# Attention stores in one written order with the loads, turns in two other slots of a quad, and two tiles turned in the next layer

## The chip, the cores and the metric

The kernel runs on one core of a Trainium2 chip. The metric is the device time of one execution in microseconds (us), the median of several runs. A core has five engines with queues of their own: TensorE (PE, matmuls and transposes; PEld is its weight load), VectorE (DVE), ScalarE (ACT), GpSimd (POOL) and SyncE (SP, which here only issues DMAs). Results of PE land in PSUM, from where DVE and ACT copy them on.

## The reference

Two kinds of layer alternate on an x of 2048 rows and 640 columns, twice each:

```python
x = x + Re(DFT_seq(DFT_hidden(LN(x))))                # spectral, layer 0
x = x + (softmax(mask(q @ k.T * 20**-0.5)) @ v) @ wo  # attention, layer 0; q, k, v from LN(x) @ wqkv
x = ...spectral, layer 1;  x = ...attention, layer 1
```

Attention has 32 heads of 20 columns; a row sees itself and the 255 rows before it. The DFTs are matmuls with given cosine and sine matrices, of which only the real part is kept.

## The kernel before, in words

**Numbers.** Float32 values are held as two f16 parts, high and low; a product of two such values takes three matmuls (high·high, high·low, low·high).

**The program** is `spectral(0)`, `attention(0)`, `spectral(1)`, `attention(1)`. The 2048 rows make 16 tiles of 128. Attention works in 8 blocks of 256 queries (two tiles), each with 16 pairs of heads and two tiles, so 32 steps to a block and 256 to a layer. Four steps are a *quad* (four heads of both tiles). `attention` is written as one loop over g, the step (from L1220 on); r is its place in the block, 0 to 31.

**One step g** issues, in this order: `scores(g)` (PE into PSUM `sp`, then DVE a masked copy L1050 and a maximum L1054 into `m`); `by_key(g−7)` (the scores of an earlier step by key into `tp`, a sigmoid on ACT L1098 into `ptq`, masks on POOL); the loads of x rows for the norm of block b+2 at r = 4; `copy_tops` (ACT L1075); one step of a layer norm on DVE (`slow_step`; its last operation is L150, into `lny`, which ACT and POOL then split into `xs`); every fourth step `values` (PE into `pv`) and every fourth `back` (the quad's output, transposed back and divided, DVE L1146 and L1147, into `os` by POOL); and then *fill*.

**Fill** is a list of generators (`Unit`) that give one matmul at a time: the q/k projection of the next block (`proj_qk`), its v projection, the output projection of the block before last (`out_tile`), and at the end of layer 0 the first stage of the next spectral layer. `run_fill(ns)` issues matmuls worth ns nanoseconds. How many a step gets is a rate times a factor by g % 4 (1.12, 0.28, 1.3 and 1.3 for 0, 1, 2 and 3).

**Turns.** A tile must be transposed before it can be contracted. A *turn* is one Unit: `turned` (L941) issues five PE transposes into the PSUM bank `pt`, and then one copy out of it, by ACT (L950) for the high part (k = 0) and by DVE (L948) for the low part (k = 1). There are three kinds: `rows_turn` (a normed tile for the projections, `xs` to `early`), `out_turn` (an attention output, `os` to `ot`), and, in layer 0, `next_turn` (a finished, normed tile for the next spectral layer, `xs` to `xto`, which is then stored to `xud`). `turn_unit()` issues one whole turn. Before, it stands at the start of the fill of each step with g % 4 = 3 and, if fill and credit are over `TURN_ROOM` = 1000 ns, of each step with g % 4 = 0.

**One bank.** `pt` has one buffer. It is also what `hand_on` uses, at the very end of each step with g % 4 = 0: four transposes of the quad's maxima (`pt<-idh,tops`), which ACT copies in the next two steps.

**Order.** Inside attention, `tensor()` (L115) chains all PE instructions in written order, and `load()` (L164 to L171) chains the DMAs issued by SP in theirs. DMAs issued by ACT (`nc.scalar.dma_start`) are not in that chain: the stores of a finished tile to `x3d` (layer 0, `next_layer`, L896) or `out` (layer 1, `out_tile`, L880), and the store of a turned tile to `xud` (L956). SP's chain holds the stores of the projected q and k to `qkd`, the loads of the stacks `ks` and `qs` from there, and the loads of x rows (`x2d`). The q/k projection of a block ends at r = 20 to 23 of the block before; its stacks are loaded directly after.

**The seam.** In layer 0 the turns of tile 15 are not queued as fill. `attention` returns them as `hidden.rest`, and `spectral(1)` runs them beside its first products (one small step of each such generator after each product).

Of the kernel before, what the change touches and what calls it, by code (L numbers as in the profile page):

```python
# [19 lines left out]
NT = S // P  # L20
# [22 lines left out]
HAND_LAG = 4  # L43
# [3 lines left out]
M_UP = 2.0 ** 15  # L47
SHIFT = -20.0
TURN_STEPS = 8
TURN_ROOM = 1000  # L50
NORM_STEPS = (4, 9)
ROW_STEPS = 3
X_UP = 2.0 ** 10
# [8 lines left out]
def body(ctx: ExitStack, tc: tile.TileContext, x_in, cmat, whid, wqkv, wo, out):  # L62
    nc = tc.nc
# [35 lines left out]
    xu_d = [dram.tile([P, 2 * ND * P], F16, name=f"xud{i}") for i in range(NT)]  # L99
# [61 lines left out]
    def split(hi, lo, y, eng):  # L161
        nc.scalar.activation(hi, y, AF.Copy)
        eng.tensor_tensor(lo, y, hi, op=OP.subtract)
# [3 lines left out]
    def load(out, in_):  # L167
        with ExitStack() as order:
            if in_turn[0] and loads:
                order.enter_context(tc.issue_after(loads[-1]))  # L170
            i = nc.sync.dma_start(out, in_)  # L171
        loads.append(i.ins)
# [9 lines left out]
    def new_f():  # L182
        return pf_.tile([P, 512], F32, tag="f", name="pf", bufs=2)
# [578 lines left out]
    def attention(layer, proj, dst, final):  # L762
        with ExitStack() as st:
# [58 lines left out]
                yield 136  # L822

            def out_turn(i, k):
                if k == 0:
                    X2[i] = keep.tile([P, D], F32, tag="res", name="x3", bufs=4)
                    load(X2[i], x2_d[i])
                    OT[i] = sb.tile([P, 2, ND, P], F16, tag="ot", name="ot", bufs=2)
                yield from turned(OS[i // 2][:, :, i % 2], k, OT[i])
                done.add((i, k))  # L830
# [31 lines left out]
            def out_tile(i):  # L862
                ot = OT[i]
                x3 = x2 = X2.pop(i)
                for n in range(2):
                    cs = slice(n * 320, (n + 1) * 320)
                    pf = new_f()
                    k = 0
                    for dt in range(ND):
                        for l, r in ((0, 0), (0, 1), (1, 0)):  # L870
                            matmul(pf[:, :320], ot[:, l, dt], bo[r][:, dt, cs], start=k == 0, stop=k == 14)
                            k += 1
                            if k < 15:
                                yield 136
                    nc.vector.scalar_tensor_tensor(x3[:, cs], pf[:, :320], beta, x2[:, cs], op0=OP.mult, op1=OP.add)  # L875
                    if n == 0:
                        yield 136
                done.add((i, 2))
                if final:
                    nc.scalar.dma_start(dst[i], x3)  # L880
                else:
                    yield from next_layer(i, x3)

            slow, live = deque(), deque()

            def new_xs():

                while len(live) > 1:
                    for g in live.popleft():
                        for _ in g:  # L890
                            pass
                live.append([])
                return keep.tile([P, 2, D], F16, tag="xs", name="xs", bufs=2)

            def next_layer(i, x3):
                nc.scalar.dma_start(dst[i], x3)  # L896
                slow.append(next_norm(i, x3))
                yield from ()

            def next_norm(i, x3):  # L900
                ys = []
                yield from norm_steps([x3], ys)
                xs = new_xs()
                split(xs[:, 0], xs[:, 1], ys[0], nc.gpsimd)
                xt = keep.tile([P, 2, ND, P], F16, tag="xto", name="xto", bufs=2)
                live[-1].extend(next_turn(i, xs, xt, k) for k in range(2))
                if i < NT - 1:
                    fill.extend(Unit(now[0] + TURN_STEPS, g, "turn", now[0], [], True) for g in live[-1])

            def split_wo():  # L910
# [29 lines left out]
            def turned(xs, k, o, d0=0, d1=ND):  # L940
                pt = new_turn()  # L941
                ptv = pt.bitcast(F16)[:, :ND * P].rearrange("p (a b) -> p a b", a=ND)
                for dt in range(d0, d1):
                    transpose(ptv[:, dt], xs[:, k, dt * P:(dt + 1) * P], idh)
                    if dt < d1 - 1:
                        yield 56
                if k:
                    nc.vector.tensor_copy(o[:, k, d0:d1], ptv[:, d0:d1])  # L948
                else:
                    nc.scalar.activation(o[:, k, d0:d1], ptv[:, d0:d1], AF.Copy)  # L950
                yield 56

            def next_turn(i, xs, xt, k):
                yield from turned(xs, k, xt)
                if k:
                    nc.scalar.dma_start(xu_d[i], xt.rearrange("p a b c -> p (a b c)"))  # L956

            OS, OT, X2, done = {}, {}, {}, set()
            lastd = [0]
            credit = [0.0]  # L960
# [39 lines left out]
            def run_fill(ns):  # L1000
                credit[0] += ns
                while credit[0] > 0:
                    if unit[0] is None:
                        unit[0] = next_unit(False)
                        if unit[0] is None:
                            credit[0] = 0.0
                            break
                    if not step(unit[0]):
                        unit[0] = None
# [159 lines left out]
            NG = NT * NP  # L1169
# [30 lines left out]
            for g in range(NS):  # L1200
                now[0] = g
                b, r = divmod(g, 2 * NP)
                if g < NG:
                    if r == 0:
                        flush(("qk", b))
                        flush(("rows", b + 1))
                        if b < NBQ - 1:
                            queue_qk(b + 1)
                            queue_v(b + 1)
                    scores(g)  # L1210
                    if g % 4 == 3:
                        part_tops(g // 4)
                if 0 <= g - KEY_LAG < NG:
                    by_key(g - KEY_LAG)
                if g < NG and b < NBQ - 2:
                    if r == NORM_STEPS[0]:
                        x2s = [keep.tile([P, D], F32, tag="res", name="x2", bufs=4) for t in range(2)]
                        for t in range(2):
                            load(x2s[t], x2_d[2 * (b + 2) + t])
                    if r == NORM_STEPS[1]:  # L1220
                        slow.append(rows_norm(b + 2, x2s))
                if g < NG and r == VALUE_LAG:
                    flush(("v", b))
                    if b < NBQ - 2:
                        proj.new_rows(b + 2)
                    if b == NBQ - 1 and not final:
                        hidden = Hidden(xu_d)
                        hidden.load()
                        for k in range(2):
                            hidden.fetch(k)  # L1230
                            fill.append(Unit(g + NEXT_STEPS[k], hidden.stage(k, None), "next", NG + k))
                for pi in range(2):
                    n, m = divmod(g - HAND_LAG - 1 - pi, 4)
                    if m == 0 and 0 <= n < NG // 4:
                        copy_tops(n, pi)
                slow_step()
                n, m = divmod(g - VALUE_LAG, 4)
                if m == 0 and 0 <= n < NG // 4:
                    for part in range(2):
                        values(n, part)  # L1240
                n, m = divmod(g - BACK_LAG, 4)
                if m == 0 and 0 <= n < NG // 4:
                    back(n)
                rate = (total - spent[0] - credit[0]) / max(NG + FILL_LAST - g, 1)
                if g < NG and r < VALUE_LAG:
                    rate = max(rate, left(("v", b)) / (VALUE_LAG - r))
                if g < NG and r < QK_SLOT:
                    rate = max(rate, left(("v", b), ("qk", b + 1)) / (QK_SLOT - r))
                ns = max(rate, 400) * FILL[(g - VALUE_LAG + 2) % 4]
                m = (g - HAND_LAG) % 4  # L1250
                if m == 3 or m == 0 and credit[0] + ns > TURN_ROOM or g >= NG + HAND_LAG:
                    turn_unit()
                run_fill(ns)
                n, m = divmod(g - HAND_LAG, 4)
                if m == 0 and 0 <= n < NG // 4:
                    hand_on(n)
# [5 lines left out]
                    slow_step()  # L1262
            in_turn[0] = False
            if not final:
                hidden.rest = chain(*live[-1])
                return hidden

    hidden = Hidden(None)
    proj = spectral(0, [x_in[i] for i in range(NT)], hidden, True)
    hidden = attention(0, proj, x3_d, False)  # L1270
# [27 lines left out]
```

## Time and profile before

| | us |
|---|---|
| runs before | 2310.66, 2311.68, 2321.39 (median 2311.68) |
| profiled execution | 2304.6 |
| its span | 2302.9 (1.7 less) |
| mean granted PE clock | 0.985 of full speed |
| attention of layer 0 | about 600 to 1204 |
| spectral layer 1 | about 1215 to 1725 |
| attention of layer 1 | about 1725 to 2303 |

In a row of a timeline stand start, duration, engine, line, operation, output<-inputs, shape, type and count, and in brackets how long the engine was idle before it and what it waited for. A row of the waits names engine, output, line, the thing waited for, and then the total, the number of waits and the longest. In rows of windows stand start:end, length, the busy time of PE, PEld, DVE, ACT and POOL, the granted PE clock, and the DMA share and rate. L numbers are those of the kernel before.

### The profile page before, as it was taken

To read this page: it belongs to the slowest core of one execution; us is meant where nothing else is said; L and a number is where in the kernel's file an instruction comes from. 1 tells how busy PE (TensorE), PEld (TensorE's weight loads), DVE (VectorE), ACT (ScalarE), POOL (GpSimd) and SP (SyncE) were. 2 spreads that over 40 slices of the span, in tenths; PEclk is the share of its full clock that TensorE was granted. 3 is DMA by queue.
4 is the path that set the end of the run, shared out by engine and by line. 5 is a ranking of instruction groups with operands and counts; after the bars stand their busy time and mean duration, and the time that the engine had idled before them with its cause. 6 is when DMAs were issued, how large, how long until landed. Compare 5 with 4: busy or idle time off the path is not lost.

```text
span 2302.9 us, 55101 instructions
## 1 busy us (share of the span) xinstructions
PE 2135.0 (93%) x21985; PEld 1499.2 (65%) x21985; DVE 1695.3 (74%) x3601; ACT 1264.4 (55%) x2120; POOL 1365.2 (59%) x1773
## 2 busy tenths in 40 slices
PE   7989899999899999999889999999998999899997
PEld 5667566667566666666556777777665666666664
DVE  7887969777678788787656758585867777577664
ACT  5334344343477777777654433434325677667775
POOL 5675758658355565455446858585754555455443
PEclk9999999999999999999899999999999999999999
DMA  5864746354432332233324545363652322332230
GB/s 187 286 213 142 233 141 218 136 220 138 128 88 65 82 86 76 73 84 94 129 76 152 182 138 200 118 210 123 249 146 74 83 62 69 77 91 55 57 88 24
DMA packets 187606, 292.95 MB, mean 127 GB/s; under 512 B 13908, under 2 KB 120660, under 8 KB 178004
## 3 DMA queue, kind: packets, MB, share of 16 engines
q1 hardware_dynamic: 157108, 223.55, 32.9%
q10 hardware_dynamic: 30240, 65.88, 7.7%
q8 instruction: 172, 2.82, 0.5%
q14 instruction: 86, 0.70, 0.1%
HBM read 202.51 MB, written 86.87 MB: 126 GB/s over the span
## 4 chain that ended last, share of the span: by engine, by line
PE 64%; DVE 20%; DMA 5%; issue 5%; ACT 3%; POOL 2%; SPq 0%; DVEq 0%; ACTq 0%; POOLq 0%
PE pf L115 25%; PE y L115 9%; PE pv L115 8%; PE z L115 6%; PE x L115 6%; PE sp L115 5%; DVE cc L485 5%; DVE m L1054 3%; PE tp L115 3%; DVE sp L1050 2%; PE pt L115 2%; DMA qs<-qkd 1%; DVE res L508 1%; ACT ptq L1098 1%; DVE lnt L146 1%
## 5 line engine op out<-in xcount | busy, mean ns | idle before, releaser
L115 PEld LDWEIGHTS <-cc 128*128 128x128 f16 x5376 | 526.8, 98 | 243.0 <-issue 39.6
L1098 ACT ACTIVATE ptq<-tp,shift,alpha 128x768 f32<-128x768 f32 (+2 forms) x512 | 485.9, 949 | 200.8 <-PE tp L115 176.4
L115 PEld LDWEIGHTS <-big 128*128 128x128 f16 x4320 | 409.4, 98 | 136.1 <-issue 26.3
L1054 DVE TENSOR_REDUCE m<-sp 128x2 f32<-128x512 f32 (+1 forms) x512 | 345.0, 674 | 17.1
L1050 DVE COPY_PREDICATED sp<-mask,sp 128x256 f32<-128x256 int32 x448 | 190.9, 426 | 221.5 <-PE sp L115 207.3
L1103 POOL TENSOR_SCALAR_AFFINE_SELECT ptq<-ptq 128x512 f32<-128x512 f32 x224 | 145.3, 649 | 300.7 <-ACT ptq L1098 300.4
L115 PE MATMUL pf<-early,big 128*128 128x256 f16 x2400 | 304.6, 273 | 0.0
L482 ACT ACTIVATE cc<-cs 128x512 f16<-128x512 f32 x256 | 152.3, 623 | 253.5 <-POOL cs L475 103.9
L115 PE MATMUL y<-zc,cc 128*128 128x320 f16 x1728 | 266.6, 302 | 14.3 <-DVE pf L508 14.1
L115 PE MATMUL pf<-big 128*128 128x320 f16 x1680 | 241.2, 301 | 10.0 <-DVE zc L253 5.5
L485 DVE SCALAR_TENSOR_TENSOR cc<-cs,cc 128x512 f16<-128x512 f32 x256 | 233.6, 928 | 3.7 <-ACT cc L482 3.5
L485 DVE SCALAR_TENSOR_TENSOR cc<-cq,cc 128x512 f16<-128x512 f32 x192 | 203.1, 1059 | 0.0
L1105 POOL TENSOR_SCALAR_AFFINE_SELECT ptq<-ptq 128x512 f32<-128x512 f32 x256 | 163.2, 638 | 43.7 <-ACT ptq L1098 43.7
L115 PE MATMUL pv<-ptq,v 128*32 128x128 f32 (+1 forms) x3840 | 188.2, 336 | 0.0
L115 PE MATMUL z<-zc,cc 128*128 128x320 f16 x1152 | 177.8, 299 | 9.2 <-DVE res L508 9.2
L115 PE MATMUL sp<-ks,qs 62*128 62x256 f16 (+1 forms) x1792 | 155.3, 250 | 31.4 <-DVE m L1054 18.4
L115 PE MATMUL x<-zc,cc 128*128 128x320 f16 x1152 | 181.4, 301 | 0.0
L115 PE MATMUL pf<-big,early 128*128 128x320 f16 x960 | 159.9, 302 | 0.8 <-DVE x L875 0.8
L115 PE MATMUL tp<-qs,ks 62*128 62x128 f16 x2688 | 151.7, 218 | 3.4 <-ACT ptq L1098 3.0
L1075 ACT ACTIVATE qs<-pt 2x512 f16<-2x512 f16 x224 | 130.9, 585 | 39.7 <-PE pt L115 36.8
L115 PE MATMUL pf<-bo,ot 128*128 128x320 f16 x840 | 144.3, 304 | 6.7 <-DVE ot L948 6.5
L115 PEld LDWEIGHTS pv<-ptq,v 128*32 128x32 f32 x3840 | 109.3, 112 | 57.8 <-issue 4.5
(144 smaller groups left out, 3525.8 us busy)
## 6 DMA issues: line engine op xcount, KB each, us to landing
cq<-in_cmat_dram SPq DMA_DIRECT2D x64, 1024.0 KB
accd<-res ACTq DMA_DIRECT2D x96, 320.0 KB
res<-accd SPq DMA_DIRECT2D x96, 320.0 KB
x<-x2d SPq DMA_DIRECT2D x64, 320.0 KB
qkd<-early SPq DMA_DIRECT2D x160, 128.0 KB
ks<-qkd SPq DMA_DIRECT2D x108, 160.0 KB
qs<-qkd SPq DMA_DIRECT2D x84, 160.0 KB
x2d<-res ACTq DMA_DIRECT2D x32, 320.0 KB
```

Source lines behind the costliest of these rows:

```text
L115: i = getattr(nc.tensor, what)(*args, **kw)
L146: nc.vector.scalar_tensor_tensor(g, u, 1.5, g, op0=OP.add, op1=OP.mult)
L482: nc.scalar.activation(cc[m][:, 0], f, AF.Copy, scale=C_UP)
L485: nc.vector.scalar_tensor_tensor(cc[m][:, 1], f, C_UP, cc[m][:, 0], op0=OP.mult, op1=OP.subtract)
L508: marks["dve"] = nc.vector.scalar_tensor_tensor(o, z, Y_DOWN, f, op0=OP.mult, op1=OP.add).ins
L1050: nc.vector.copy_predicated(sp[:, :, 2 * P:3 * P], mask[:, None, :].to_broadcast([P, 2, P]), far)
L1054: topped[0] = nc.vector.tensor_reduce(TOP[g // 4][:, g % 4], sp[:, :, c0:3 * P], axis=AX.X, op=OP.max).ins
L1075: nc.scalar.activation(o, handed[n][rs].rearrange("r (i p) t -> r i p t", i=2), AF.Copy)
L1098: nc.scalar.activation(q[:, h:h + 2, a0 + first:a0 + 3], tp[:, :, first * P:3 * P].rearrange("p a (b c) -> p a b c", c=P), AF.Sigmoid, bia ...
L1103: nc.gpsimd.affine_select(out=q[:, :, a0], in_=q[:, :, a0], pattern=[[0, 4], [-1, P]], base=0, channel_multiplier=1, compare_op=OP.is_gt, ...
L1105: ins = nc.gpsimd.affine_select(out=q[:, :, a0 + 2], in_=q[:, :, a0 + 2], pattern=[[0, 4], [1, P]], base=0, channel_multiplier=-1, compare ...
```

## The change

It has four parts.

1. The stores to `x3d`, `out` and `xud` during attention go through `load()`, so SP issues them, in written order with the loads. 46 DMAs move from ACT to SP (16 to `x3d`, 16 to `xud`, 14 to `out`); the last two tiles of layer 1 are stored by ACT as before.
2. `turn_unit()` stands in each step with g % 4 = 2 or 3, between two halves of the step's fill. `TURN_ROOM` is gone.
3. `out_turn` takes its residual tile and loads it at k = 1, one turn later.
4. The turns of tile 14 are, like those of tile 15, not queued as fill but handed to the next spectral layer.

```diff
             def out_turn(i, k):
-                if k == 0:
+                if k:
                     X2[i] = keep.tile([P, D], F32, tag="res", name="x3", bufs=4)
                     load(X2[i], x2_d[i])
+                else:
                     OT[i] = sb.tile([P, 2, ND, P], F16, tag="ot", name="ot", bufs=2)
...
                 if final:
-                    nc.scalar.dma_start(dst[i], x3)
+                    load(dst[i], x3)
...
             def next_layer(i, x3):
-                nc.scalar.dma_start(dst[i], x3)
+                load(dst[i], x3)
...
-                if i < NT - 1:
+                if i < NT - 2:
                     fill.extend(Unit(now[0] + TURN_STEPS, g, "turn", now[0], [], True) for g in live[-1])
...
                 if k:
-                    nc.scalar.dma_start(xu_d[i], xt.rearrange("p a b c -> p (a b c)"))
+                    load(xu_d[i], xt.rearrange("p a b c -> p (a b c)"))
...
-                m = (g - HAND_LAG) % 4
-                if m == 3 or m == 0 and credit[0] + ns > TURN_ROOM or g >= NG + HAND_LAG:
+                if g % 4 in (2, 3) or g >= NG + HAND_LAG:
+                    run_fill(ns / 2)
                     turn_unit()
-                run_fill(ns)
+                    run_fill(ns / 2)
+                else:
+                    run_fill(ns)
...
-                hidden.rest = chain(*live[-1])
+                hidden.rest = chain(*live[0], *live[1])
```

Counted in the order in which PE's instructions are written, 33 steps have a turn directly ahead of `hand_on`'s transposes before, and none after. In the last block of layer 0, 9 steps have no fill matmul before (r = 10 to 18), and 14 after (r = 9 to 22); 31 fill matmuls come later there. The end of the q/k projection stays at r = 20 to 23 of a block.

DVE, layer 0, block 2, from the end of step 83 on, before; L1050 and L1054 are the score operations that come once in a step, `lny<-x` ends a norm, and `xto<-pt` empties the bank after a turn's low part:

```order
L150 TENSOR_SCALAR lny<-x_9266,lnmv,lnt 128x640
L1050 COPY_PREDICATED sp<-mask,sp 128x2x128
L1054 TENSOR_REDUCE m<-sp 128x2
L150 TENSOR_SCALAR lny<-x_9267,lnmv,lnt 128x640
L948 COPY xto<-pt 128x640
L1050 COPY_PREDICATED sp<-mask,sp 128x2x128
L1054 TENSOR_REDUCE m<-sp 128x2
```

The same place after:

```order
L149 TENSOR_SCALAR lny<-x_9272,lnmv,lnt 128x640
L1050 COPY_PREDICATED sp<-mask,sp 128x2x128
L1054 TENSOR_REDUCE m<-sp 128x2
L149 TENSOR_SCALAR lny<-x_9273,lnmv,lnt 128x640
L1050 COPY_PREDICATED sp<-mask,sp 128x2x128
L1054 TENSOR_REDUCE m<-sp 128x2
L1050 COPY_PREDICATED sp<-mask,sp 128x2x128
L1054 TENSOR_REDUCE m<-sp 128x2
L948 COPY xto<-pt 128x640
```

The copy has moved from the quad's first step, in which the maxima are handed on through the same bank, two steps on, to the third.

SP, layer 1, around the end of a block's q projection (`qkd_0` is its q, `qkd_1` the next k; `qs` and `ks` are the stacks; `x` are x rows), before:

```order
L171 DMA qkd_0_157<-early 128x2x256 x5
L171 DMA qs<-onesd_164 2x4096 x2
L171 DMA qs<-qkd_0_157 20x16x256 x6
L171 DMA x_29232<-x2d_86 128x640
L171 DMA x_29267<-x2d_93 128x640
L171 DMA x_29268<-x2d_94 128x640
L171 DMA qkd_1_160<-early 128x2x256 x3
```

The same place after:

```order
L170 DMA qkd_0_157<-early 128x2x256
L170 DMA x_28585<-x2d_85 128x640
L170 DMA qkd_0_157<-early 128x2x256 x4
L170 DMA qs<-onesd_164 2x4096 x2
L170 DMA qs<-qkd_0_157 20x16x256 x6
L170 DMA out_dram<-x_28585 128x640
L170 DMA x_29110<-x2d_86 128x640
L170 DMA x_29273<-x2d_93 128x640
L170 DMA x_29274<-x2d_94 128x640
L170 DMA out_dram<-x_29110 128x640
L170 DMA qkd_1_160<-early 128x2x256 x5
```

The stores of two finished tiles now stand among the loads, one directly behind the query stack, one ahead of the next block's k stores, and a residual tile's load has moved among the q stores.

DVE at the end of attention of layer 0, before; `lnt` and `lny` belong to the norms of tiles 14 (x_16994) and 15 (x_17209), `cc` to the conversion of the next layer's matrices, `big` and `zc` are results of its first stage:

```order
L150 TENSOR_SCALAR lny<-x_16994,lnmv,lnt 128x640
L146 SCALAR_TENSOR_TENSOR lnt<-lnt 128x1
L485 SCALAR_TENSOR_TENSOR cc<-cq,cc 128x512
L142 SCALAR_TENSOR_TENSOR lnt<-lnt 128x1
L485 SCALAR_TENSOR_TENSOR cc<-cs,cc 128x512
L146 SCALAR_TENSOR_TENSOR lnt<-lnt 128x1
L485 SCALAR_TENSOR_TENSOR cc<-cs,cc 128x512
L150 TENSOR_SCALAR lny<-x_17209,lnmv,lnt 128x640
L485 SCALAR_TENSOR_TENSOR cc<-cs,cc 128x512 x2
L948 COPY xto<-pt 128x640
L485 SCALAR_TENSOR_TENSOR cc<-cq,cc 128x512
L253 SCALAR_TENSOR_TENSOR big<-pf,big 128x320 x3
```

The same place after, from tile 14's norm (x_16974) on:

```order
L149 TENSOR_SCALAR lny<-x_16974,lnmv,lnt 128x640
L130 BN_AGGR lnmv<-lnst 128x2
L948 COPY xto<-pt 128x640
L134 TENSOR_SCALAR lnt<-lnmv 128x1
L252 SCALAR_TENSOR_TENSOR zc<-pf,zc 128x320
L135 TENSOR_SCALAR lnt<-lnt 128x1
L484 SCALAR_TENSOR_TENSOR cc<-cq,cc 128x512
L136 TENSOR_SCALAR lnt<-lnt 128x1
L137 TENSOR_SCALAR lnt<-lnt 128x1
L484 SCALAR_TENSOR_TENSOR cc<-cq,cc 128x512
```

Tile 14's norm ends ahead of the conversions `cc`, which stood ahead of it before, and no copy of tile 14 follows it there.

More of the change, by code (lines that the diff above doesn't have):

```diff
@@ L49 @@
 TURN_STEPS = 8
-TURN_ROOM = 1000
 NORM_STEPS = (4, 9)
```

## Prediction, made before the changed kernel ran

> **What bounds the kernel now.** The page's first lines and its chain of waits come first.
>
> ```profile
> span 2302.9 us, 55101 instructions
> PE 2135.0 (93%) x21985; PEld 1499.2 (65%) x21985; DVE 1695.3 (74%) x3601; ACT 1264.4 (55%) x2120; POOL 1365.2 (59%) x1773
> PE 64%; DVE 20%; DMA 5%; issue 5%; ACT 3%; POOL 2%; SPq 0%; DVEq 0%; ACTq 0%; POOLq 0%
> ```
>
> TensorE (PE) is busy for 93% of the span and no matmul is taken away. So the change can be worth only PE's idle time, 2302.9 − 2135.0 = 168 us over the whole program, and what PE does at a lower clock. Which of that idle time does it touch? The waits of PE in the attention of layer 0 (640 to 1120 us), columns: total, times, longest:
>
> ```profile
> PE pt L115 <- DVE xto L948: 9.5, 8, 2.3
> PE sp L115 <- DVE m L1054: 6.1, 11, 1.1
> PE pt L115 <- ACT early L950: 3.9, 7, 0.8
> PE pt L115 <- ACT xto L950: 2.2, 4, 1.3
> PE pt L115 <- ACT ot L950: 2.0, 4, 0.6
> PE pt L115 <- DVE ot L948: 0.9, 1, 0.9
> PE pt L115 <- DVE early L948: 0.7, 1, 0.7
> PE sp L115 <- DMA qs<-qkd: 0.5, 1, 0.5
> ```
>
> The largest group is the single PSUM bank `pt`: a turn's transposes or those of the maxima wait until the copy of the turn before has emptied it. In the attention of layer 1 (1740 to 2220 us) there are no `xto` turns, and other rows stand first:
>
> ```profile
> PE sp L115 <- DMA qs<-qkd: 7.3, 3, 5.6
> PE sp L115 <- DMA x<-x2d: 3.9, 1, 3.9
> PE pt L115 <- ACT early L950: 1.0, 4, 0.4
> ```
>
> There the scores of a block wait for its stack of queries. So the two layers have different limits beside PE's own work, and the change has a part for each. (±0.5% is 11.6 us here, about what a measurement of this kernel can tell from no change.)
>
> **The stores, layer 1.** The stall's place, the timelines of SP, ACT and PE and SP's waits:
>
> ```profile
> 1978.25 11.17 SPq L171 DMA_DIRECT2D qs<-qkd  x6
> 1983.88 0.34 ACTq L880 DMA_DIRECT2D out_dram<-x  x1
> SPq L171 <- DMA out_dram<-x: 8.8, 1, 8.8
> 1991.68 0.28 PE L115 MATMUL sp<-ks,qs 62*128 62x256 f16 x1 [1.31 <-DMA qs<-qkd]
> 1997.55 0.37 PE L115 MATMUL sp<-ks,qs 62*128 62x256 f16 x2 [5.59 <-DMA qs<-qkd]
> 2072.07 0.37 PE L115 MATMUL sp<-ks,qs 62*128 62x256 f16 x2 [3.95 <-DMA x<-x2d]
> 2131.89 2.75 SPq L171 DMA_DIRECT2D qs<-qkd  x6
> ```
>
> SP begins six loads at 1978.25 and needs 11.17 us to issue them, 8.8 of these waiting for the store of a finished tile, which ACT issues only at 1983.88, between sigmoids. At the undisturbed block boundary (last row) the same six take 2.75 us and no score waits. The loads don't read what the store writes; in the built program an SP transfer waits for the one before it on the same completion semaphore, and that one was ACT's. With the stores in SP's own written order, the store stands where its data are long ready and nothing on SP can wait for an issue that ACT is late with. The 7.3 and 3.9 us go: **−11.2 us** (ends 0 and −11.2). The loads end some 13 us before PE needs them (1978.25 to 1991.68) once they are issued without a pause, so nothing else is late next.
>
> The clock after these two stalls, in columns PE busy, PEld, DVE, ACT, POOL, granted clock, DMA share, GB/s:
>
> ```profile
> 1997.00:2001.00 4.00, 3.45 (x29) 2.36 (x29) 1.16 (x3) 1.47 (x2) 1.22 (x2) 0.50 0.31 118
> 2001.00:2006.00 5.00, 5.00 (x69) 2.84 (x63) 2.20 (x4) 3.39 (x6) 0.52 (x1) 0.80 0.01 3
> 2072.00:2077.00 5.00, 4.92 (x48) 3.19 (x52) 2.24 (x4) 3.15 (x4) 1.22 (x2) 0.50 0.19 70
> 2077.00:2082.00 5.00, 5.00 (x60) 3.02 (x53) 2.41 (x6) 2.78 (x5) 1.22 (x2) 0.89 0.00 0
> 1115.00:1140.00 25.00, 18.32 (x213) 11.10 (x211) 14.18 (x38) 14.24 (x19) 10.18 (x17) 0.73 0.53 216
> ```
>
> After the first stall 4 us pass at 0.50 and 5 at 0.80, a loss of 0.50×4 + 0.20×5 = 3.0 us of PE's work; after the second 0.50×5 + 0.11×5 = 3.05. Together 6.05 at most, if PE were all that counts there; DVE's share of the chain is 20%, so I take **−4** (0 to −6). The Trainium skill, "TensorE: Matmul & The Clock Gate", Part 1, says that the clock is halved after about 3.4 us without work and restored after about as long of busy time. The trace agrees in kind (0.50 behind waits of 5.59 and 3.95 us, 0.80 and 0.89 a window later), so these microseconds hang on the two stalls and not on the steps that show them.
>
> What speaks against this: the Trainium skill, "DMA: Bandwidth & Descriptors", section "Issuing engines are not separate DMA queues", says that DMAs of all issuing engines share the same 16 DMA engines and that the choice of engine only saves issue time on the sequencer. By that rule the two terms above are nothing; the trace has the 8.8 us wait on a store of the other engine against it. It makes a rival below. The issue time itself: 46 stores of 0.34 us (row 1983.88) leave ACT, 15.6 us, and come onto SP. ACT ends 3% of the chain and SP's issuing 0%, so I cost both at nothing.
>
> **The turns, layer 0.** Step 84 of layer 0, where the turn stands first in the step and the maxima's transposes last:
>
> ```profile
> 769.37 0.45 PE L115 MATMUL pt<-idh,xs 128*128 128x128 f16 x5
> 770.95 1.61 DVE L150 TENSOR_SCALAR lny<-x,lnmv,lnt 128x640 f32<-128x640 f32 x1
> 772.48 0.48 DVE L948 COPY xto<-pt 128x640 f16<-128x640 f16 x1
> 773.01 0.38 PE L115 MATMUL pt<-idh,tops 128*66 128x128 f16 x4 [2.34 <-DVE xto L948]
> ```
>
> The turn's five transposes end at 769.82. DVE gets to the copy only at 772.48, behind the block's norm, and PE waits 2.34 us with its whole queue: the next scores are written behind the maxima. In the new order no turn stands in a step that hands maxima on (33 such steps before, none after, counted in the written order); the copy has a step and more (some 1.8 us) before the bank is wanted. The rows of `xto`, `ot` and the one DVE row of `early` add to 9.5 + 2.2 + 2.0 + 0.9 + 0.7 = 15.3. The 3.9 of `early` by ACT partly stays, since turns of one block's rows are flushed one behind the other at block ends. Best end: 15.3 + 3.9 = −19. Worst end: waits come back at the new places, since now two turns stand in neighbouring steps (slots 2 and 3) and DVE's queue is no shorter: I put half of 15.3, −8. I take **−15**: what is late next is the score's PSUM bank (`DVE m`, 6.1 for 11 waits), and it is late in steps without turns already.
>
> **The last two tiles, the seam of the layers.** PE, DVE and ACT there:
>
> ```profile
> 1203.94 0.44 PE L115 MATMUL pt<-idh,xs 128*128 128x128 f16 x5
> 1208.73 0.69 DVE L485 SCALAR_TENSOR_TENSOR cc<-cq,cc 128x512 f16<-128x512 f32 x1
> 1210.17 0.74 ACT L162 ACTIVATE xs<-lny 128x640 f16<-128x640 f32 x1 [0.49 <-DVE lny L150]
> 1210.96 0.71 PE L115 MATMUL pt<-idh,xs 128*128 128x128 f16 x5 [4.98 <-DVE lnt L142]
> 1212.86 0.71 PE L115 MATMUL pt<-idh,xs 128*128 128x128 f16 x5 [1.19 <-POOL xs L163]
> 1214.77 0.29 PE L115 MATMUL pf<-idh,xs 128*128 128x128 f16 x1 [1.20 <-ACT xs L162]
> 1214.85 1.54 PE L115 MATMUL pf<-big 128*128 128x320 f16 x5
> ```
>
> PE transposes tile 14 by itself (waits of 4.98 and 1.19), then waits 1.20 for tile 15, and the products start at 1214.85. After the change no tile is turned behind 13; the first turn in the products' stretch needs tile 14's `xs` only, ready at 1210.17 + 0.74 = 1210.91. So the products start 1214.85 − 1210.91 = 3.9 us earlier, and tile 14's norm now stands ahead of the chunk conversions on DVE, of which one (0.69) was in front: 4.6 together, **−4.6** (0 if tile 15's norm ends last in either order; best −7.4, all three waits). Against it, tile 14's ten transposes now stand between products: 2 × 0.44 = **+0.9**.
>
> **What the moves cost.** Layer 0's last block has 14 steps without fill after, 9 before (counted in the written order); the 31 matmuls that these held are issued later. The window 1115 to 1140 us has the clock at 0.73: 0.27 × 25 = 6.75 us lost already. Five steps more of nine could lengthen that: **+2** (0, because the matmuls fill other gaps; +6, because the low clock doubles). The Trainium skill, same page as above, Part 4, says that transposes don't count as PE work for the clock gate. If so the steps with turns alone stay at the low clock; no run here shows it, and it would push this term to its upper end.
>
> The residual tile's load, one turn later, is wanted only behind the turn and 15 matmuls: 0 (up to +3, if a few of the 30 tiles wait).
>
> **Sum:** −11.2 − 4 − 15 − 4.6 + 0.9 + 2 = −31.9. Against the profiled execution of 2304.6 us (span 2302.9 and 1.7 around it) that is 2272.7; the median of the runs is 2311.68, 7.1 above the profiled one, and the same difference gives 2279.8, about 2280. With the terms at their best ends (−11.2 − 6 − 19 − 7.4 + 0.9) the difference is −42.7, 2269; with turns, seam and last block at their worst ends (−11.2 − 4 − 8 + 0.9 + 6) it is −16.3, 2295.
>
> **Rivals.** *A: SP's order holds loads back, slower.* A store in written order that waits for its data holds everything behind it on SP; in layer 0 the stores of turned tiles (`xud`) stand right ahead of the key loads of a block. If such a store waits more than the 13 us by which loads are early, scores wait: at each of 6 boundaries 5.6 us and 3.0 of clock, as measured for the one stall: 6 × 8.6 = +51.6, together −31.9 + 51.6 = +19.7, 2331. For it: exactly such a chain costs 8.8 us now. Against it: the store's data is a copy of 0.48 us behind a turn (row 772.48), 13 us is many steps, and layer 0's only wait on a query load is 0.5. *B: the stalls stay*, as by the rule above, since the loads share DMA engines with the same bytes: the first two terms fall, −31.9 + 15.2 = −16.7, 2295. Against it the two boundaries, 11.17 us with a late store and 2.75 without. *C: the turn waits change their name.* If DVE is what is late in these steps, PE waits at the next score for `m` instead of for `xto`; of the −15 only −3 stays: −19.9, 2292. For it DVE's 20% of the chain and 1.61 us for one norm operation in the row of step 84; against it, PE fills the time with fill matmuls that need no DVE. *D: nothing measurable*, turns and stores both only push the waits along: 2304 to 2312.
>
> **How the numbers follow.** Forecast 0.60; A 0.05, B 0.12, C 0.15, D 0.08. The likeliest case gives 2280. The range holds forecast, B and C: below, the sum of best ends, 2269, less the 1 us by which the two close runs differ: 2268; above, B with the turns at their worse end (−16.7 + 7 = −9.7), 2302. Left out are A, D and tails, about 2 in 10. Faster by over 0.5%: forecast, B and C, 0.87; within: D, 0.08; slower: A, 0.05.
>
> **What would show it.** Right: SP has no wait on `out_dram` and the six query loads of every boundary in layer 1 take about 3 us; PE's waits on `qs` in 1740 to 2220 are under 1 us and the clock stays high there; in layer 0 the rows `pt <- xto` and `ot` fall below 3 us together, with `DVE m` about as before; products start within some 2 us of tile 14's split. Wrong: waits on `ks` or `qs` in layer 0 (A), the 7.3 still there (B), `DVE m` grown by 10 (C), or a longer low-clock stretch at the end of either attention.

## The result, and the profile after

The changed kernel takes 2274.0 us (median of 4 runs, 2268.34 to 2283.0) beside 2311.17 for the one before: ratio 0.9848, 95% interval 0.9819 to 0.9877. Measured again beside some of its parts it took 2271.76 us, ratio 0.9816 (0.9790 to 0.9842). The profiled execution took 2268.34 us, 36.3 less than the 2304.6 of before; 31.9 less was forecast. Comparisons below leave disturbed runs out, and the profiled execution of one kernel (stores alone, clock 0.852) is not read for durations.

The page of after: PE does the same matmuls, in a shorter span. Its idle time is down from 168 to 2266.6 − 2131.3 = 135 us, its busy time by 3.7.

```profile
span 2266.6 us, 55134 instructions
PE 2131.3 (94%) x21985; PEld 1498.0 (66%) x21985; DVE 1699.9 (75%) x3601; ACT 1263.9 (56%) x2120; POOL 1364.0 (60%) x1773
PE 66%; DVE 21%; DMA 5%; issue 4%; ACT 2%; POOL 2%; SPq 0%; DVEq 0%; ACTq 0%; POOLq 0%
```

PE's waits after, layer 0, over the same steps as before (644.6 to 1112 us):

```profile
PE sp L114 <- DVE m L1054: 7.4, 18, 1.1
PE pf L114 <- DVE x L875: 5.9, 6, 1.2
PE tp L114 <- ACT ptq L1098: 2.7, 10, 0.4
PE pt L114 <- ACT early L950: 1.6, 3, 0.8
PE pf L114 <- DVE ot L948: 1.0, 1, 1.0
...
PE pt L114 <- DVE xto L948: 0.5, 1, 0.5
PE pt L114 <- DVE early L948: 0.5, 1, 0.5
```

The bank `pt` has gone from the head of the list: `xto`, `ot` and `early` together from 19.2 to 2.6 us. A new row stands second, fill that waits for the output projection's result (`x`, L875) to be read from its PSUM buffer.

The same for layer 1 (1726 to 2186 us):

```profile
PE sp L114 <- DVE m L1054: 8.0, 20, 0.9
PE pf L114 <- DVE x L875: 2.2, 3, 1.0
PE sp L114 <- DMA qs<-qkd: 1.4, 1, 1.4
```

The waits for the query stack are down from 11.2 to 1.4 us. SP's timeline at the boundary that had the long stall, and the granted clock (second number from behind, before share and rate: 1.00) just after it:

```profile
1959.89 2.77 SPq L170 DMA_DIRECT2D qs<-qkd  x6
1966.55 0.37 SPq L170 DMA_DIRECT2D out_dram<-x  x1
```

```profile
1974.00:1979.00 5.00, 5.00 (x80) 3.31 (x75) 3.08 (x6) 4.13 (x6) 1.22 (x2) 1.00 0.01 3
```

The six loads take 2.77 us where they took 11.17, the tile's store stands behind them, and PE goes on at full clock where it had 0.50.

The place of step 84, PE and DVE: the turn (777.73) now stands two steps behind the maxima (773.96), and nobody waits for the copy at 778.64.

```profile
773.96 0.39 PE L114 MATMUL pt<-idh,tops 128*66 128x128 f16 x4
777.73 0.45 PE L114 MATMUL pt<-idh,xs 128*128 128x128 f16 x5
```

```profile
778.64 0.48 DVE L948 COPY xto<-pt 128x640 f16<-128x640 f16 x1
```

The seam, PE: the last output projection ends at 1195.37 + 0.43 = 1195.80, and the products start 4.54 us later. Before, it was 10.74 (from 1204.11 to 1214.85).

```profile
1195.37 0.43 PE L114 MATMUL acc<-bo,ot 128*128 128x320 f16 x2
1196.12 0.44 PE L114 MATMUL pt<-idh,xs 128*128 128x128 f16 x5 [0.31 <-DVE xto L948]
1197.57 0.44 PE L114 MATMUL pt<-idh,xs 128*128 128x128 f16 x5 [1.01 <-ACT xto L950]
1199.21 0.69 PE L114 MATMUL x<-early,cc 128*128 128x320 f16 x2 [1.20 <-DVE lnt L134]
1200.34 4.20 PE L114 MATMUL pf<-big 128*128 128x320 f16 x15
```

So the predicted signs are there, but for the wait on `qs`: 1.4 us, where under 1 was the sign (0.4 in the second profile). They don't tell which part of the change brought what, and the experiments changed that picture.

### The profile page after: what moved, and what is told of

It reads as the page before. It is cut to its first block, busy times and chain, and to the rows that moved or that the text cites. A ratio compares the mean times of both kernels' runs of the same rounds, so it can differ in the third digit from the quotient of the medians.

```text
span 2266.6 us, 55134 instructions
## 1 busy us (share of the span) xinstructions
PE 2131.3 (94%) x21985; PEld 1498.0 (66%) x21985; DVE 1699.9 (75%) x3601; ACT 1263.9 (56%) x2120; POOL 1364.0 (60%) x1773
## 4 chain that ended last, share of the span: by engine, by line
PE 66%; DVE 21%; DMA 5%; issue 4%; ACT 2%; POOL 2%; SPq 0%; DVEq 0%; ACTq 0%; POOLq 0%
PE pf L114 26%; PE y L114 9%; PE pv L114 8%; PE z L114 6%; PE x L114 6%; PE sp L114 5%; DVE cc L484 5%; DVE m L1054 3%; PE tp L114 3%; DVE sp L1050 2%; PE pt L114 2%; DVE res L507 1%; DVE lnt L145 1%; DMA x2d<-res 1%; DVE lny L149 1%
## 5 line engine op out<-in xcount | busy, mean ns | idle before, releaser
L1054 DVE TENSOR_REDUCE m<-sp 128x2 f32<-128x512 f32 (+1 forms) x512 | 345.1, 674 | 17.2
L1050 DVE COPY_PREDICATED sp<-mask,sp 128x256 f32<-128x256 int32 x448 | 190.6, 426 | 183.6 <-PE sp L114 168.3
L114 PE MATMUL pf<-early,big 128*128 128x256 f16 x2400 | 313.3, 273 | 0.0
L1075 ACT ACTIVATE qs<-pt 2x512 f16<-2x512 f16 x224 | 130.9, 585 | 38.3 <-PE pt L114 36.3
L114 PEld LDWEIGHTS <-ks 62*128 62x128 f16 x3008 | 116.1, 94 | 42.7 <-DVE m L1054 20.0
```

Of the source, the lines that this page charges most:

```text
L114: i = getattr(nc.tensor, what)(*args, **kw)
L1050: nc.vector.copy_predicated(sp[:, :, 2 * P:3 * P], mask[:, None, :].to_broadcast([P, 2, P]), far)
L1054: topped[0] = nc.vector.tensor_reduce(TOP[g // 4][:, g % 4], sp[:, :, c0:3 * P], axis=AX.X, op=OP.max).ins
L1075: nc.scalar.activation(o, handed[n][rs].rearrange("r (i p) t -> r i p t", i=2), AF.Copy)
```

## The experiments

All kernels were timed in several rounds beside the kernel before. The three columns on the right are from each one's profile: attention of layer 0 and of layer 1, from the first score maximum (DVE L1054) to the last, and the *seam*, from layer 0's last maximum to the 13th accumulator store of the next spectral layer. In the names: 1 stores, 2 turn slots, 3 late residual load, 4 tile 14.

| kernel | us | ratio (95% interval) | attention 0 | seam | attention 1 |
|---|---|---|---|---|---|
| before | 2311.17 | 1 | 565.96 | 154.24 | 540.17 |
| changed (1+2+3+4) | 2274.0 | 0.9848 (0.9819–0.9877) | 547.47 | 155.00 | 518.82 |
| the same again | 2271.76 | 0.9816 (0.9790–0.9842) | 547.61 | 152.62 | 520.79 |
| 1 alone | 2297.8 | 0.9947 (0.9927–0.9968) | | | |
| 1 alone, in layer 1 only | 2294.24 | 0.9927 (0.9912–0.9941) | 565.49 | 154.24 | 526.87 |
| 2 alone | 2265.94 | 0.9807 (0.9787–0.9827) | 547.24 | 153.26 | 519.26 |
| 4 alone | 2305.24 | 0.9987 (0.9972–1.0002) | 566.53 | 150.63 | 540.26 |
| 1+2 | 2262.61 | 0.9788 (0.9761–0.9814) | 544.44 | 157.36 | 516.38 |
| 1+2+4 | 2264.32 | 0.9805 (0.9791–0.9820) | 544.45 | 152.66 | 519.40 |
| 2+3+4 | 2268.55 | 0.9805 (0.9780–0.9830) | 549.90 | 152.20 | 518.19 |
| new slots, turn ahead of fill | 2268.01 | 0.9806 (0.9782–0.9831) | 544.15 | 154.48 | 523.23 |
| old slots, turn amid fill | 2312.7 | 1.0005 (0.9994–1.0017) | 573.25 | 153.43 | 538.90 |
| 2 + three tiny loads | 2301.01 | 0.9960 (0.9945–0.9976) | 544.19 | 153.29 | 551.58 |
| changed + three tiny loads | 2270.68 | 0.9814 (0.9795–0.9833) | 547.63 | 152.86 | 518.06 |

My theory: late stores hold SP (layer 1), the single bank holds PE (layer 0), and each part of the change takes one of the two away. The rivals: the choice of queue matters only by its issue time; the turn waits only change their name.

**The stores alone.** The kernel before with these three edits:

```diff
-                    nc.scalar.dma_start(dst[i], x3)
+                    load(dst[i], x3)
...
-                nc.scalar.dma_start(dst[i], x3)
+                load(dst[i], x3)
...
-                    nc.scalar.dma_start(xu_d[i], ...)
+                    load(xu_d[i], ...)
```

> The kernel before with the stores alone on SP in written order. Theory (a load on SP waits for a store that ACT issues late): in the attention of layer 1 PE's waits of 7.3 and 3.9 us on qs and x go and with them about 6 us of half clock, so layer 1 is 13 to 18 us shorter; layer 0 keeps its 9.5 us on xto and gains nothing; in all 2294 to 2299 beside 2311. Rival B (the choice of issuing engine saves only issue time): the waits on qs stay and the time is within 4 us of before. Rival A (SP's order holds loads back): PE waits on ks or qs appear in layer 0, slower.

It is faster, ratio 0.9947. The rival by issue time falls.

**The stores of layer 1 alone** (the first of the three edits):

> The kernel before with the stores of layer 1 alone on SP in order (layer 0's x3d and xud stay on ACT). Theory: layer 1's attention loses its 11.2 us of waits and about 6 us of low clock, 15 to 18 us shorter by its steps, layer 0 is unchanged; ratio 0.992 to 0.995, at least as good as all stores (0.9947). If layer 0's stores cost something in SP's order, this one is 3 to 5 us faster than all stores.

Attention 0 is unchanged, and attention 1 is 13.3 us shorter. From its second block on, which leaves out the first block's extra clock loss of this execution, it is 16.7 us shorter: the 11.2 us of waits, and 5.5 that are put down to the clock (PE's busy time for the same matmuls there fell by 5.7 us, from 455.95 to 450.23). PE's waits there (1741 to 2208 us), with no row for `qs`, and in layer 0 (640 to 1120), where the bank stands first as before:

```profile
PE sp L115 <- DVE m L1054: 7.8, 17, 1.0
PE pf L115 <- DVE ot L948: 2.6, 2, 2.2
```

```profile
PE pt L115 <- DVE xto L948: 9.5, 8, 2.4
```

So the stores in SP's order are enough to end the stall. Whether layer 0's stores cost something there (0.9947 with them, 0.9927 without) the intervals leave open.

**The turn slots alone:**

```diff
-                m = (g - HAND_LAG) % 4
-                if m == 3 or m == 0 and credit[0] + ns > TURN_ROOM or g >= NG + HAND_LAG:
+                if g % 4 in (2, 3) or g >= NG + HAND_LAG:
+                    run_fill(ns / 2)
                     turn_unit()
-                run_fill(ns)
+                    run_fill(ns / 2)
+                else:
+                    run_fill(ns)
```

> The kernel before with the turn slots alone. Theory (the single bank): in layer 0 the waits on pt by xto, ot and early copies, 20 us in all, fall to under 4 us, attention 0 is 10 to 15 us shorter net of some longer waits on m and x; layer 1 keeps the stalls on qs. In all 2294 to 2301 beside 2311. Rival C (the waits change their name): waits on m rise by 10 us and the time is within 5 us of before.

This is the surprise: 0.9807, as much as the whole change, and attention 1 is as short as with everything (519.26). The stores are still ACT's. PE's waits in layer 1 (1722 to 2182 us), SP's waits in the whole attention of layer 1, and SP and ACT at the boundary that had the stall:

```profile
PE sp L115 <- DVE m L1054: 8.9, 20, 0.9
PE tp L115 <- ACT ptq L1098: 1.2, 4, 0.4
PE sp L115 <- DMA x<-x2d: 1.1, 1, 1.1
```

```profile
SPq L171 <- DMA out_dram<-x: 45.1, 6, 9.1
```

```profile
1957.68 3.19 SPq L171 DMA_DIRECT2D qs<-qkd  x6
1968.74 1.29 SPq L171 DMA_DIRECT2D x<-x2d  x3
```

```profile
1963.88 0.34 ACTq L880 DMA_DIRECT2D out_dram<-x  x1
```

SP waits for late stores as long as before (45.1 us; before it was 47.2 in 6 waits), yet PE hardly waits (1.1 us). The wait now falls on the x load *behind* the six query loads. In the built programs, the DMAs of SP and ACT take eight completion semaphores in turn (in the trace of before, 974 issues on eight semaphores, 121 or 122 on each), and a transfer of SP waits for the eighth one before it. Before, the eighth behind two of the layer's stores was one of the six query loads of a stack, at the two boundaries that stalled: the store at 1983.88 shares its semaphore with the load issued at 1987.36, the store at 2061.64 with the one at 2063.82. With the new slots the output tiles end elsewhere, and the eighth is never a query load; at four boundaries it is the x load just behind them (the store at 1963.88, the load at 1968.74).

**Three tiny loads.** If that is the whole cause, moving the count by three must bring the stall back. To the slots alone, in layer 1, three loads of 32 bytes into a tile that nobody reads are added between the rows of ones and the six loads of a query stack (`now_layer[0]` is 1 in layer 1):

```diff
+        if w == 0 and b and now_layer[0]:
+            for k in range(3):
+                load(ones[32 * k:32 * k + 2, 0, 8 * b:8 * b + 8], ones_d[0][:, :8])
         for pi in range(2):
             for r, part in enumerate(...):
```

> The kernel before with the turn slots alone (ratio 0.981), and in layer 1 three added loads of 32 bytes between the rows of ones and the six loads of each query stack, so that the eighth DMA behind ACT's store is the fourth of the six and no longer an x load. Theory (an SP transfer waits for the eighth one before it, whoever issues that): SP waits 5 to 9 us on out_dram among the query loads of up to 6 blocks, PE waits for qs or for the last load again, 2 to 5 us each and 1 to 3 us of clock: 10 to 40 us slower than the slots alone, ratio 0.985 to 0.998. Rival (the stalls were only the loads' share of the DMA engines, or the slots' earlier projection): three tiny loads change nothing, within 4 us of 0.981.

The ratio goes from 0.9807 to 0.9960, and attention 1 from 519.26 to 551.58 us. SP's waits in layer 1's attention, SP and ACT at one boundary, PE's waits (1724 to 2213 us), a score of PE that waits, and the clock at one of the stalls:

```profile
SPq L172 <- DMA out_dram<-x: 67.5, 7, 17.1
```

```profile
1963.41 10.49 SPq L172 DMA_DIRECT2D qs<-qkd  x6
```

```profile
1969.51 0.34 ACTq L884 DMA_DIRECT2D out_dram<-x  x1
```

```profile
PE sp L116 <- DMA qs<-qkd: 23.1, 5, 7.5
```

```profile
2129.27 0.37 PE L116 MATMUL sp<-ks,qs 62*128 62x256 f16 x2 [5.76 <-DMA qs<-qkd]
```

```profile
2128.00:2133.00 5.00, 3.73 (x27) 2.45 (x29) 1.12 (x2) 1.66 (x3) 1.23 (x2) 0.50 0.14 36
```

The six loads take 10.49 us again, around a store of ACT, and in the trace six of the layer's stores now share their semaphore with a query load. The 32.3 us by which attention 1 is longer are 23.1 of waits less the 1.1 there was, and some 10 for the lower clock after the stalls: PE's busy time in attention 1 rose by 10.0 us (500.41 to 510.38). The control, the changed kernel with the same tiny loads:

> The changed kernel with the same three tiny loads. Its stores are issued by SP in order, so the eighth DMA back is never a late one: within 4 us of the changed kernel (ratio 0.982), PE waits under 3 us on qs in layer 1. If tiny loads by themselves cost (their issue, their 32-byte packets), this one is slower by as much as the other.

Ratio 0.9814, attention 1 518.06: with the stores in SP's order nothing happens. The tiny loads cost nothing measurable by themselves.

**The stores back on ACT** in the changed kernel (2+3+4):

> The changed kernel with the stores back on ACT, out of SP's order. Theory as predicted (late stores hold the query stacks): about 15 us slower than the changed kernel. Theory after the runs of the parts (the new turn slots alone already move the ACT stores behind the stack loads in the written order, so nothing is left to gain for the stores): within 4 us of the changed kernel, SP still waits some 45 us on out_dram in layer 1, but ahead of x loads, and PE waits under 2 us on qs.

0.9805: behind the new slots the stores gain nothing that can be measured. What they are worth shows only where the count falls badly, as in the kernel before and with the tiny loads.

**Slots or halves?** Two versions take the edit on turns apart. The new slots with the turn ahead of the whole fill:

```diff
-                m = (g - HAND_LAG) % 4
-                if m == 3 or m == 0 and credit[0] + ns > TURN_ROOM or g >= NG + HAND_LAG:
+                if g % 4 in (2, 3) or g >= NG + HAND_LAG:
                     turn_unit()
                 run_fill(ns)
```

> The kernel before with turns in steps g % 4 = 2 and 3, but ahead of the fill, not between its halves. If the slots do it (the bank is not wanted by the maxima), within 4 us of the slots with halves, 2262 to 2270. If the halves matter (a turn right behind the score matmuls waits for the bank or DVE), waits on pt by xto, ot and early in layer 0 are 5 to 10 us and the time is 2272 to 2280.

And the old slots with the turn between halves:

```diff
                 if m == 3 or m == 0 and credit[0] + ns > TURN_ROOM or g >= NG + HAND_LAG:
+                    run_fill(ns / 2)
                     turn_unit()
-                run_fill(ns)
+                    run_fill(ns / 2)
+                else:
+                    run_fill(ns)
```

> The kernel before with turns in their old steps (g % 4 = 3 and 0), but between the halves of the fill. Theory (the slot is what counts: in the first step of a quad the bank is wanted by the maxima at the end): PE's waits on pt by xto and ot in layer 0 are as long or longer (10 to 20 us), the time is 0 to 10 us above before. If the halves were what helps, waits on pt fall below 5 us and the ratio is 0.98 to 0.99.

The first is as fast as with halves (0.9806), the second no faster than before (1.0005). PE's waits in the second, layer 0 (643 to 1133 us):

```profile
PE pt L115 <- DVE xto L948: 6.1, 4, 2.4
PE sp L115 <- DVE m L1054: 4.8, 8, 1.1
PE pt L115 <- ACT early L950: 3.9, 7, 0.8
PE pt L115 <- ACT xto L950: 3.7, 6, 1.3
PE tp L115 <- ACT ptq L1098: 3.5, 12, 0.7
PE pt L115 <- ACT ot L950: 3.4, 4, 1.6
```

The bank is waited for much as before; the slot counts, the halves don't. In the traces a turn stands between a step's scores and the transposes of the maxima in 33 steps before, in 34 with the old slots amid the fill, and in none with the new slots. Layer 1 shows the same: its stalls stay in the second version (1742 to 2282 us) and are absent from the first.

```profile
PE sp L115 <- DMA qs<-qkd: 11.0, 3, 5.3
```

**Tile 14 alone:**

```diff
-                if i < NT - 1:
+                if i < NT - 2:
...
-                hidden.rest = chain(*live[-1])
+                hidden.rest = chain(*live[0], *live[1])
```

> The kernel before with tile 14 alone handed to the next layer. Theory: from the last xs transposes of attention 0 to the first product of the next layer 3 to 5 us less, of which 1 is lost again at the first accumulator store; 2306 to 2309 beside 2311. If the longer tail of attention 0 that the changed kernel shows (36.97 to 40.74 us from the last score step to the last turns) belongs to this edit, the tail grows here too and the gain is under 1 us; if to the turn slots, the tail stays at 37.

By the times it can't be told from nothing (0.9972 to 1.0002). In the trace the seam is 3.6 us shorter (154.24 to 150.63), and the products start 6.92 us after the last output projection, not 10.74. The stretch from the last maximum to that projection's end grew little (37.14 to 38.69), so its growth in the changed kernel (42.68, in its second profile 41.15) is mostly not this edit's. It goes with the stores joined to the slots: the five kernels with both have 41.15 to 42.68, the four with the new slots and ACT's stores 38.44 (the slots alone) to 40.40. Where both are in, PE waits 3.0 us for ACT's copy of an output turn (1.07 with the slots alone), and the clock of the stretch is 0.92 in the changed kernel and 0.96 in the other four (1.00 before and with the slots alone). The row of the changed kernel:

```profile
1162.64 0.33 PE L114 MATMUL pt<-idh,os 128*128 128x128 f16 x3 [3.00 <-ACT ot L950]
```

Why ACT is late there wasn't tried further. Behind slots and stores the edit itself is worth 4.7 us of seam: 157.36 without it (1+2) and 152.66 with it (1+2+4). The times of these two don't show it.

**The late residual load undone** (1+2+4):

> The changed kernel with the residual tile loaded at the first turn again. Theory: no wait depends on it, within 4 us of the changed kernel (2274). Rival: with the stores in SP's order an earlier load must wait for its buffer, which frees when a store on the same queue ends, and holds the stacks behind it: waits on qs or ks return, 5 to 9 us slower than the changed kernel for each.

And slots and stores without parts 3 and 4 (1+2), beside the changed kernel again:

> The kernel before with stores in SP's order and the turn slots, no late residual load, tile 14 turned as before. If the stores are worth nothing behind the slots and tile 14 about 3 us: 2264 to 2270 (ratio 0.980 to 0.983). If the parts added up (-12 and -44): 2254.

> The changed kernel again, beside its parts. If the residual tile's late load costs nothing, it is within 4 us of the version with the early load (2264.3 beside 2309.6, ratio 0.9805); if the late load costs what the first runs suggest, 2270 to 2276 (ratio 0.983 to 0.986).

The medians with the early load, 2264.3 and 2262.6, lie under the 2271.8. Their intervals overlap with that of the changed kernel's second measurement; with the first (0.9819 to 0.9877) one just touches and the other doesn't. In the traces attention 0 is 3.2 us shorter with the early load (547.61 to 544.45 and 544.44). The row `pf <- DVE x L875`, 5.9 us in the changed kernel, is shorter in the version with the early load (644.6 to 1112 us there, too; of its rows only this one is shown):

```profile
PE pf L114 <- DVE x L874: 2.9, 3, 1.2
```

The row is 5.9 in all four kernels with the new slots and the late load, and 1.8 to 3.1 in the five with the new slots and the early one. So part 3 costs some 3 us by the traces, too little for the times to show surely. (One execution scatters by as much: the slots alone and the slots with the tiny loads are the same program in layer 0, and have 547.24 and 544.19.) The version with the slots and the stores, 0.9788 (0.9761 to 0.9814), has the lowest ratio; the slots alone, 0.9807, can't be told from it.

## Why the prediction was right, and where its reasons were not

**Layer 0's turns and last block** (−15 and +2). From the first maximum to the end of the last output projection it was 603.10 us (601.01 to 1204.11) and is 590.15 (605.65 to 1195.80): −13.0, as summed. The mechanism is shown by the two versions of slots and halves. That the sum is met so closely is luck, since its terms were off and cancelled. Waits on `pt` fell by 16.6 us, but the new row of 5.9 on `x` (some 3 to 4 of it from part 3) and longer ones on `m` (6.1 to 7.4) and `ptq` (1.1 to 2.7) gave half of that back: rival C held for a part, mostly with other names than `m`. Over these steps the kernel is 12.6 us shorter all the same (480.0 to 467.4 us), as PE's idle time fell from 30.9 to 21.4 and its busy time from 449.1 to 446.1. With the slots alone the whole stretch is 585.68, 17.4 shorter than before; the four kernels with part 3 and the new slots have 588.8 to 590.2. On the other side the last block didn't cost +2: it is 6.0 us shorter between its maxima, and the stretch after it is 5.5 longer, of which 1.3 comes with the slots alone and the rest with the stores beside them (under tile 14). The low-clock stretch inside the block got better (0.73 before), but there is now another in the stretch after it, so that this sign of being wrong is there for a part:

```profile
1112.00:1137.00 25.00, 20.61 (x312) 13.72 (x311) 17.16 (x42) 18.53 (x26) 9.68 (x18) 0.92 0.26 94
```

**Layer 1's stall** (−11.2 and −4). The waits went nearly as sized, 11.2 to 1.4. The clock term was too small: 5.5 us with the stores alone, inside the ends (0 to −6) and near −6. PE was what counted there, and a share of the chain was a poor reason to cut it. Attention 1 as a whole is 21.4 us shorter, for which the prediction had 15.2. Besides the clock it had no term for a turn in layer 1: a wait of 2.17 us for a turned output tile, with a clock of 0.89 and 0.76 around and behind it. Its list of layer 1's waits leaves out this row (`pf` on DVE's `ot`, 2.6 in all) and the one on `m` (7.0). The stores alone leave this wait as it was (2.17 again); with the new slots it is gone, and also with the old slots and the turn amid the fill, so it hangs on where the turn stands:

```profile
1828.13 0.72 PE L115 MATMUL pf<-bo,ot 128*128 128x320 f16 x4 [2.17 <-DVE ot L948]
```

```profile
1825.00:1830.00 5.00, 2.83 (x27) 1.69 (x27) 4.11 (x10) 2.37 (x4) 4.41 (x7) 0.89 0.06 19
1830.00:1835.00 5.00, 5.00 (x66) 3.06 (x65) 1.64 (x4) 2.95 (x5) 1.22 (x2) 0.76 0.50 117
```

The step of the prediction that failed is the attribution: "With the stores in SP's own written order" the stalls go. They do, but they go with the turn slots alone too, since the wait then falls on a load with time to spare. So rival B's case, in which the turns are gained and the stalls stay, could not have come about: with the slots in place the stalls go even if the stores stay ACT's. Counting which DMA stands eighth behind each store, for each part by itself, would have shown that.

The margin of "some 13 us" was mis-sized as well: it counts from the first of the six issues. They end at 1978.25 + 11.17 = 1989.42, and the score waits until 1997.55, 8.1 us more. The changed kernel shows the same at its last boundary, 7.5 us from the end of the issues to the score:

```profile
2168.70 2.93 SPq L170 DMA_DIRECT2D qs<-qkd  x6
2179.16 0.28 PE L114 MATMUL sp<-ks,qs 62*128 62x256 f16 x2 [1.39 <-DMA qs<-qkd]
```

With 2.75 us of undisturbed issue and some 8 behind it, my estimate is that about 3 of the 13.4 us were spare.

**What the issuing engine is worth.** The Trainium skill ("DMA: Bandwidth & Descriptors", section "Issuing engines are not separate DMA queues") says that issuing DMAs on several engines saves only issue time. For a store among loads that isn't all here: moving 14 stores of layer 1 alone was worth 13 to 17 us with the same bytes. The measurement decides: what counts is what SP's next transfers wait for.

**The seam** (−4.6 + 0.9). From the last output projection to the products it is 10.74 − 4.54 = 6.2 us shorter, nearer to the best end. The products' stretch up to the 13th store takes 1.4 us more (106.36 to 107.78), where 0.9 was put. Alone the edit gave −3.6 net, behind slots and stores −4.7. That the whole seam is hardly shorter than before, if at all (155.00 and 152.62, before 154.24), is due to the longer stretch between the last maximum and the last output projection.

**The residual load** (0, up to +3): the upper end, by the trace.

**Rival A** (SP's order holds stacks back) didn't come. SP does wait for the data of a store in its order, in layer 1 88.8 us in all and up to 24.4, in layer 0 (605 to 1160 us) 70.3 and, for turned tiles, 27.4. But PE's waits in layer 0 have no row for a load, and in layer 1 none for `ks` and only 1.4 us for `qs`, where SP had waited for the last store of q itself (2.1 us). So no stack was held too long by a tile's store. Layer 1:

```profile
SPq L170 <- DVE x L875: 88.8, 10, 24.4
```

The total came near because attention 0 and the waits of layer 1 were sized from their own rows, and in part by luck. It was 4.4 us short against the profiled run: −6.2 in layer 1 and −1.1 at the seam and its stretch, against some +4.6 in the first spectral layer, whose code didn't change (its end went from 601.01 to 605.65; 602.11 in the second profile), so that this last piece is scatter; the rest lies in pieces of about 1 us.

## What to carry to other kernels

When a queue waits for another engine's late DMA, ask which of its own transfers the wait lands on: waits of 45 us cost 1.1 us of PE's time here ahead of loads with slack, and waits of 47 and 67 us cost 17 and 32 where some fell among the loads of a stack that was soon to be read; three DMAs more or less decided it. Gains of two edits that end the same stall don't add; test each alone. A buffer that two users share in a fixed rhythm is best filled by one of them soon after the other has emptied it, so that its copy has a step's time: here the slots alone took 17.4 us out of the attention of layer 0.

## What was not expected of the hardware and its program

Three loads of 32 bytes per query stack made the kernel 35 us slower (2265.94 to 2301.01) by their number, not by their bytes: beside stores in one order they cost nothing that can be measured (2271.76 and 2270.68). And of the 47.2 us that SP waited for late stores in layer 1, two waits of six reached PE; with the clock's loss behind each stall these were worth 16.7 us.
